# The products of a feed-forward block: from seven-for-eight float32 products to three float32r products of split parts

## The chip, the cores and the metric

The kernel runs on one core of a Trainium2 chip. The metric is device time in microseconds (us) from the start of the program to its end, the median of several executions. The core has a matrix engine (TensorE, in the profile PE, with its weight loads as PEld), a vector engine (VectorE, DVE), a scalar engine (ScalarE, ACT), a general engine (GpSimd, POOL) and a queue that issues most of the transfers (SyncE, SP). Each engine takes its own instructions strictly in the order in which they were written; engines wait for each other through semaphores.

## The reference

```
attn_out = mamba2_ssd(x, a, B, C)       # (4, 8, 768, 32): batch, heads, tokens, head dim
x = attn_out.transpose(0, 2, 1, 3).reshape(3072, 256)
h = maximum(maximum(x @ w1, x @ w2), x @ w3)     # w: 256 x 768
return h @ w_out                                 # w_out: 768 x 256
```

The first line is a decaying state-space scan with a state of 16 per head, in float32. The other lines are a feed-forward block (FFN) with a maximum over three products. The four FFN weights arrive as float64, so the kernel reads each as two 32-bit words per value and puts a float32 together from them ("decoding").

## The kernel before, in words

The 768 tokens of each batch are cut into six blocks of 128; with four batches a block has 4 x 128 = 512 columns (`BLK`). Blocks are called 0 to 5 here (`c` in the code). The program is unrolled and its order is written out by hand: `tc.manual_schedule()` keeps every instruction where the code puts it, and the strings `FIRST` (block 1), `STEADY` (blocks 2 to 4) and `LAST` (block 5) are plans of one word per action. While the FFN of block c runs, the plan weaves the scan of block c+1 between its products: transposes of B and C, scores (`s`), their product with the decay matrix L (128x512 multiplies on VectorE, in the list `later`, run by a digit in the plan), exponentials of L on ScalarE (words with x and z), masks of L on GpSimd (m and n), the state (A) and the scan's output y.

The FFN of block 0 uses plain float32 products of the three weights with `yT`, 512 columns each, while the weights are still being fetched and decoded. `decode()` begins with one weight part (two ScalarE, two VectorE, one GpSimd operation), `sign()` ends it (VectorE).

From block 1 on the code uses max(a1, a2, a3) = a2 + max(a1 - a2, a3 - a2, 0). `weight_sums` replaces w1 and w3 by their differences to w2 (`DIFF`, `BASE`); the a2 part goes through w2 and w_out at once: `fold_base` multiplies w2 by w_out into a 256x256 matrix, and the down product adds y times that matrix (`terms`). For the two differences, six pairs of weight columns (q = 0 to 2, i = 0 or 1) are each multiplied with y by a seven-for-eight (Strassen) scheme: `early` makes four products of 256 columns in PSUM banks sumA and sumB and the sums that follow, `late` three more, and the maxima. `weight_sums` and `scan_sums` prepare the sums of weights and of y that the seven products need.

`down_next` makes a quarter of the down product of half a block per call: for a group of 128 tokens eight terms (six of h with w_out, two of y with the folded matrix), 256 columns each; two groups share a bank, ScalarE copies it and SP sends it off. The down steps of block c run during block c+1, and the last block's are made by `last_next` at the end.

The words of a plan that matter here: E and L are early and late, D a down step, l a step of the last block's, a digit takes that many multiplies from `later`, y makes the scan's output, g and G turn and fold w2.

Of the kernel before, what the change touches and what calls it, by code (L numbers as in the profile page):

```python
# [11 lines left out]
U32 = mybir.dt.uint32  # L12
AF = mybir.ActivationFunctionType
# [6 lines left out]
def kernel(  # L20
# [39 lines left out]
    HB = BLK // 2  # L60
    MASKED = -32768.0
# [4 lines left out]
    raw = ctx.enter_context(tc.tile_pool(name="raw", bufs=2))  # L66
    att = ctx.enter_context(tc.tile_pool(name="att", bufs=2))
    ffn = ctx.enter_context(tc.tile_pool(name="ffn", bufs=2))
    wraw = ctx.enter_context(tc.tile_pool(name="wraw", bufs=10))
    wtmp = ctx.enter_context(tc.tile_pool(name="wtmp", bufs=3))  # L70
# [3 lines left out]


# [6 lines left out]
    def sum_bank(kind, shape):  # L82
        return bank("sum" + kind, {"A": 1, "B": 2}[kind], shape, "sum" + kind)

    def att_bank(shape, name):
        turn["att"] += 1
        if shared["att"] and turn["att"] % 5 == 0:
            return bank("sumA", 1, shape, name)
        return bank("att", 4, shape, name)

    def ffn_bank(shape, name):
        turn["ffn"] += 1
        if shared["ffn"] and turn["ffn"] % 3:
            return bank("sumB", 2, shape, name)
        return bank("ffn", 1, shape, name)

# [25 lines left out]
    def load(c, name):  # L122
        src, w = sources[name]
        t = blocks[c][name] = raw.tile([P, BH, w], FP32, tag="raw_" + name, name="raw_" + name)
        nc.sync.dma_start(
            out=t, in_=src[:, :, c * P:(c + 1) * P, :].rearrange("b h s n -> s (b h) n"))
# [3 lines left out]
    w_sb = [const.tile([P, KD, DF], FP32, name="w%d" % i) for i in range(3)]  # L130
    wo_sb = const.tile([P, NF, DM], FP32, name="wo")
# [5 lines left out]
    weight_jobs = []  # L137
    for f0 in range(0, DF, WCOL):
        for w, t in zip((moe_w1, moe_w2, moe_w3), w_sb):
            per = 1 if w.dtype == FP32 else 2  # L140
            src = words(w)[:, per * f0:per * (f0 + WCOL)]
            weight_jobs.append(
                (t[:, :, f0:f0 + WCOL], src.rearrange("(k p) f -> p k f", p=P), w.dtype))
    for o in range(0, NF, 2):
        weight_jobs.append(
            (wo_sb[:, o:o + 2],
             words(moe_w_out)[o * P:(o + 2) * P, :].rearrange("(o p) m -> p o m", p=P),
             moe_w_out.dtype))
# [3 lines left out]
    def fetch():  # L152

        dst, src, dt = weight_jobs.pop(0)
        if dt == FP32:
            nc.sync.dma_start(out=dst, in_=src)
        else:
            rb = wraw.tile([P, 2, WCOL, 2], U32, tag="rb", name="rb")
            nc.sync.dma_start(out=rb.rearrange("p k f w -> p k (f w)"), in_=src)
            fetched.append((dst, rb))  # L160

    def decode_steps():


        dst, rb = fetched.pop(0)
# [4 lines left out]
        def first():  # L170
# [3 lines left out]
            held["u"] = u = wtmp.tile(shape, U32, tag="w_u", name="w_u")  # L174
# [8 lines left out]
            r = wtmp.tile(shape, U32, tag="w_r", name="w_r")  # L183
# [3 lines left out]
        def second():  # L187
            nc.vector.scalar_tensor_tensor(  # L188
                out=dst.bitcast(U32), in0=hi.rearrange("p (k f) -> p k f", k=2),
                scalar=0x80000000, in1=held["u"].rearrange("p (k f) -> p k f", k=2),  # L190
                op0=ALU.bitwise_and, op1=ALU.bitwise_or)
# [184 lines left out]
    def last_load(c):  # L376
        E = blocks[c]["E"] = raw.tile([HN, NB, P], FP32, tag="E", name="E")
# [22 lines left out]
    def scan_b(c, kind):  # L400
# [4 lines left out]
        st["BT"] = BT = att.tile([HN, NB, P], FP32, tag="BT", name="BT")  # L405
# [13 lines left out]
    def scan_c(c):  # L419
# [3 lines left out]
        st["CT"] = CT = att.tile([HN, NB, 2, P], FP32, tag="CT", bufs=1, name="CT")  # L423
# [7 lines left out]
    def scan_cd(c):  # L431
# [3 lines left out]
        st["Cd"] = Cd = att.tile([HN, NB, P], FP32, tag="Cd", name="Cd")  # L435
        nc.vector.tensor_tensor(out=Cd, in0=st["trC"], in1=E, op=ALU.mult)

    def scan_bd(c):
        st = blocks[c]
        st["Bd"] = Bd = att.tile([P, BH, N], FP32, tag="Bd", name="Bd")  # L440
# [83 lines left out]
    def first_own(bs):  # L524
# [9 lines left out]
        if 0 not in yT:  # L534
            yT[0] = ffn.tile([P, KD, BLK], FP32, tag="yT", bufs=3, name="yT")
# [3 lines left out]

    def scan_y(c):  # L540
        yT[c] = ffn.tile([P, KD, BLK], FP32, tag="yT", bufs=3, name="yT")
        for t in range(KD):
            nc.scalar.copy(out=yT[c][:, t], in_=blocks[c]["y"][t].rearrange("p b i -> p (b i)"))

    def scan_sums(c):

        y11, y12, y21, y22 = (
            yT[c][:, k, r * HB:(r + 1) * HB] for k in range(2) for r in range(2))
        late = [blocks[c]["y"][k].rearrange("p b i -> p (b i)")[:, r * HB:(r + 1) * HB]
                for k in range(2) for r in range(2)]  # L550
        t = ysum[c % 2]
        later.extend(
            lambda k=k, a1=a1, a0=a0: nc.vector.tensor_tensor(
                out=t[:, k], in0=a1, in1=a0, op=ALU.subtract)
            for k, (a1, a0) in enumerate((
                (late[1], y11), (late[3], t[:, 0]), (late[3], y12), (late[2], t[:, 1]))))
        sides[c] = {1: y11, 2: y21, 3: y22, 4: t[:, 3], 5: t[:, 0], 6: t[:, 1], 7: t[:, 2]}


    hT = {}  # L560
    def h_of(c):
        if c not in hT:
            hT[c] = ffn.tile([P, NF, BLK], FP32, tag="h", name="h")
        return hT[c]

    def group(bank, i, f, halves):

        for r in halves:
            for k in range(KD):
                nc.tensor.matmul(  # L570
                    out=bank[:, r * HB:(r + 1) * HB],
                    lhsT=w_sb[i][:, k, f * P:(f + 1) * P],
# [3 lines left out]
    def whole_group(bank, i, f):  # L576
        for k in range(KD):
            nc.tensor.matmul(  # L578
                out=bank, lhsT=w_sb[i][:, k, f * P:(f + 1) * P], rhs=yT[0][:, k],
# [11 lines left out]
    NW = len(DIFF) * NQ  # L591
    ysum, wsum = [], {}

    def kilos(b):

        t = wraw.tile([P, 2, WCOL, 2], U32, tag="rb", name="rb").bitcast(FP32)
        return t.rearrange("p k f w -> p (k f w)").rearrange("p (a b) -> p a b", b=b)

    quarters = {}

    def places():
        for _ in range((NW + 1) // 2):
            t = kilos(P)
            for half in (t[:, 0:4], t[:, 4:8]):
                if len(wsum) < NW:
                    wsum[len(wsum)] = half
        ysum.extend(kilos(HB) for _ in range(2))

    def weight_sums(k):
        q, i = divmod(k, 2)  # L610
        w = w_sb[DIFF[i]]
        cols = slice(2 * q * P, 2 * (q + 1) * P)
        nc.vector.tensor_tensor(  # L613
            out=w[:, :, cols], in0=w[:, :, cols], in1=w_sb[BASE][:, :, cols], op=ALU.subtract)
        a11, a12, a21, a22 = (
            w[:, kk, (2 * q + g) * P:(2 * q + g + 1) * P]
            for g in range(2) for kk in range(2))
        s1, s2, s3, s4 = (wsum[k][:, j] for j in range(4))
        nc.gpsimd.tensor_tensor(out=s1, in0=a21, in1=a22, op=ALU.add)  # L619
        nc.gpsimd.tensor_tensor(out=s3, in0=a11, in1=a21, op=ALU.subtract)  # L620
        nc.gpsimd.tensor_tensor(out=s2, in0=s1, in1=a11, op=ALU.subtract)  # L621
        nc.gpsimd.tensor_tensor(out=s4, in0=a12, in1=s2, op=ALU.subtract)

    def left(p, k):
        if p in (1, 2, 4):
            q, i = divmod(k, 2)
            g, row = {1: (0, 0), 2: (0, 1), 4: (1, 1)}[p]
            f = 2 * q + g
            return w_sb[DIFF[i]][:, row, f * P:(f + 1) * P]
        return wsum[k][:, {5: 0, 6: 1, 7: 2, 3: 3}[p]]  # L630

    def products(c, k, which, first):
        for p, bank, half in which:
            nc.tensor.matmul(  # L634
                out=bank[:, half], lhsT=left(p, k), rhs=sides[c][p],
                start=(first and half == 0), stop=True, skip_group_check=True)
# [8 lines left out]
    held = {}  # L645

    def early(c, k):
        q, i = divmod(k, 2)
        A, B = (sum_bank(kind, [P, 2, HB]) for kind in "AB")
        products(c, k, [(1, A, 0), (6, A, 1), (5, B, 0), (7, B, 1)], True)  # L650
        if i == 0:
            held["m"] = ffn.tile([P, 4, HB], FP32, tag="m", name="m")

        if i > 0 and q % 2 not in quarters:
            quarters[q % 2] = kilos(HB)[:, 0:3]
        t = held["m"][:, 1:4] if i == 0 else quarters[q % 2]
        eu = wtmp.tile([P, 2, HB], FP32, tag="w_u", name="eu")
        v = wtmp.tile([P, 2, HB], FP32, tag="w_r", name="v")[:, 0]
        nc.scalar.copy(out=eu[:, 0], in_=A[:, 0])  # L659
        nc.vector.tensor_tensor(out=eu[:, 1], in0=A[:, 1], in1=eu[:, 0], op=ALU.add)  # L660
        nc.vector.tensor_tensor(out=v, in0=B[:, 1], in1=eu[:, 1], op=ALU.add)
        nc.vector.tensor_tensor(out=t[:, 2], in0=B[:, 0], in1=v, op=ALU.add)
        held["open"] = A, B, eu, t

    def late(c, k):
        q, i = divmod(k, 2)
        m = held["m"]
        A, B, eu, t = held.pop("open")
# [394 lines left out]
```

## Time and profile before

| what | us |
|---|---|
| three runs | 281.45, 283.35, 286.68 (median 283.35) |
| profiled execution, its span | 281.2 |
| TensorE busy in it | 267.4 (95%) |
| VectorE, ScalarE, GpSimd busy | 159.0, 116.6, 67.2 |
| block 0 (with the start), block 1 | 59.9, 46.4 |
| blocks 2, 3, 4 | 40.9, 40.9, 40.6 |
| block 5 with the end | 52.5 |

The time of the profiled execution itself is known by its span alone. The borders of the blocks are those between the first up products in TensorE's timeline. A line of the groups reads: line of the kernel, engine, operation, what it writes and reads, shapes, number of records; then busy time, mean duration of one in ns, idle time of the engine before them and what ended it. A float32 matmul leaves two records, one for each half of its weights. Neighbouring matmuls overlap in the records, so the cost of one is read from the distance of starts. Their mean duration is longer than that.

### The profile page before, as it was taken

How to read it: one execution, taken by the hardware profiler on the slowest of the kernel's cores; microseconds unless marked ns; L12 is line 12 of the kernel's file. 1: busy time of each engine (PE TensorE's matmuls, PEld its weight loads, DVE VectorE, ACT ScalarE, POOL GpSimd, SP SyncE). 2: the span in 40 equal slices, each digit the busy share in tenths (PEclk: the TensorE clock that was granted, in tenths of full speed). 3: DMA queues.
4: the chain of work that ended last, by engine and by line, in shares of the span. 5: the costliest groups of instructions: out<-in, count | busy, mean ns of one | idle time of the engine just before them, and what ended most of it. 6: DMA issues, size and time to landing. Idle time of an engine off the chain costs nothing.

```text
span 281.2 us, 4990 instructions
## 1 busy us (share of the span) xinstructions
PE 267.4 (95%) x1930; PEld 209.6 (75%) x1930; DVE 159.0 (57%) x298; ACT 116.6 (41%) x304; POOL 67.2 (24%) x84
## 2 busy tenths in 40 slices
PE   6889999989989999999999999999999999999994
PEld 4665344467767888877888868888878888888873
DVE  2585778989877342475643576634477534524320
ACT  2776588835756157332274332456231111100101
POOL 5163665457837400005200005100000000000000
PEclk9999999999999999997999999999999999999999
DMA  7989989989789408692005795001010001010012
GB/s 84 194 277 286 281 144 170 168 229 206 165 201 123 63 0 216 171 135 45 0 2 161 207 123 70 2 1 40 0 37 1 2 0 40 0 37 2 0 37 75
DMA packets 105047, 28.10 MB, mean 100 GB/s; under 512 B 75328, under 2 KB 101952, under 8 KB 105024
## 3 DMA queue, kind: packets, MB, share of 16 engines
q1 hardware_dynamic: 104144, 27.14, 48.4%
q10 hardware_dynamic: 880, 0.66, 0.7%
q8 instruction: 15, 0.25, 0.4%
q14 instruction: 8, 0.07, 0.1%
HBM read 24.54 MB, written 3.24 MB: 99 GB/s over the span
## 4 chain that ended last, share of the span: by engine, by line
PE 80%; DVE 13%; POOL 2%; ACT 2%; issue 2%; POOLq 0%; DVEq 0%; ACTq 0%
PE o L741 21%; PE sumB L634 16%; PE sumA L634 14%; PE up L578 6%; PE o L762 5%; PE s L483 5%; DVE L L491 4%; PE y L519 3%; PE fold L713 2%; PE y L506 1%; PE up L570 1%; PE spread L320 1%; DVE m L676 1%; DVE w_u L176 1%; DVE w L613 1%
## 5 line engine op out<-in xcount | busy, mean ns | idle before, releaser
L741 PE MATMUL o<-wo,h 128*128 128x256 f32 x240 | 58.4, 379 | 0.0
L391 ACT ACTIVATE L<-L,ncums 128x128 f32<-128x128 f32 x160 | 50.0, 392 | 7.1 <-POOL L L384 7.1
L741 PEld LDWEIGHTS o<-wo,h 128*128 128x128 f32 x240 | 45.5, 190 | 6.2
L659 ACT COPY eu<-sumA 128x256 f32<-128x256 f32 x30 | 11.2, 372 | 76.5 <-PE sumA L634 76.5
L660 DVE TENSOR_TENSOR eu<-sumA,eu 128x256 f32<-128x256 f32 x30 | 12.7, 424 | 52.5 <-ACT eu L659 52.5
L634 PE MATMUL sumA<-yT,w 128*128 128x256 f32 x120 | 37.5, 394 | 0.0
L491 DVE TENSOR_TENSOR L<-s,L 128x512 f32<-128x512 f32 x46 | 29.3, 681 | 2.9 <-PE s L483 2.9
L634 PE MATMUL sumB<-rb 128*128 128x256 f32 x120 | 30.8, 379 | 0.0
L578 PE MATMUL up<-yT,w 128*128 128x512 f32 x64 | 29.1, 600 | 0.2 <-DVE w L188 0.2
L634 PEld LDWEIGHTS sumA<-yT,w 128*128 128x128 f32 x120 | 21.7, 192 | 5.5 <-issue 1.4
L634 PEld LDWEIGHTS sumB<-rb 128*128 128x128 f32 x120 | 23.0, 192 | 3.2
L384 POOL TENSOR_SCALAR_AFFINE_SELECT L<-L 128x1024 f32<-128x1024 f32 x20 | 23.5, 1206 | 0.0
L578 PEld LDWEIGHTS up<-yT,w 128*128 128x128 f32 x64 | 11.6, 190 | 14.7 <-issue 11.7
L483 PE MATMUL s<-CT,BT 32*128 32x256 f32 x192 | 19.6, 403 | 3.1 <-DVE L L491 1.7
L185 POOL TENSOR_TENSOR w_u<-w_u,w_r 128x512 uint32<-128x512 uint32 x12 | 15.6, 1299 | 28.2 <-DVE w_u L179 14.6
L634 PE MATMUL sumA<-rb 128*128 128x256 f32 x60 | 18.4, 389 | 1.3 <-POOL rb L619 1.3
L483 PEld LDWEIGHTS s<-CT,BT 32*128 32x128 f32 x192 | 12.1, 184 | 10.0 <-issue 6.4
L634 PE MATMUL sumB<-yT,rb 128*128 128x256 f32 x60 | 18.1, 383 | 0.7 <-POOL rb L621 0.4
L634 PE MATMUL sumB<-rb,w 128*128 128x256 f32 x60 | 17.8, 379 | 0.0
L741 PE MATMUL o<-rb,yT 128*128 128x256 f32 x64 | 16.4, 379 | 0.0
L676 DVE TENSOR_TENSOR m<-sumB,eu 128x512 f32<-128x512 f32 x15 | 10.3, 688 | 10.6 <-PE sumB L634 10.5
L746 ACT COPY ob<-o 128x512 f32<-128x512 f32 x10 | 5.8, 583 | 21.6 <-PE o L741 21.6
(112 smaller groups left out, 365.8 us busy)
## 6 DMA issues: line engine op xcount, KB each, us to landing
L<-cums SPq DMA_DIRECT2D x10, 1024.0 KB, 9.3
rb<-in_moe_w_dram SPq DMA_DIRECT2D x9, 512.0 KB, 6.3
raw_x<-in_x_dram SPq DMA_DIRECT2D x6, 512.0 KB, 7.4
out_dram<-ob SPq DMA_DIRECT2D x10, 256.0 KB, 2.5
raw_B<-in_B_dram SPq DMA_DIRECT2D x6, 256.0 KB, 4.5
raw_C<-in_C_dram SPq DMA_DIRECT2D x6, 256.0 KB, 6.4
rb<-in_moe_w_out_dram SPq DMA_DIRECT2D x3, 512.0 KB, 6.1
E<-cums SPq DMA_DIRECT2D x40, 32.0 KB, 4.0
```

Source lines behind the costliest of these rows:

```text
L185: nc.gpsimd.tensor_tensor(out=u, in0=u, in1=r, op=ALU.add)
L384: nc.gpsimd.affine_select(out=Ls[c][:, b], in_=Ls[c][:, b], pattern=[[0, NH], [1, P]], compare_op=ALU.is_ge, fill=MASKED, base=0, channel_ ...
L391: nc.scalar.activation(L[:, b, h], L[:, b, h], AF.Exp, bias=ncum[c][:, b * NH + h:b * NH + h + 1], scale=1.0)
L483: nc.tensor.matmul(out=s[:, i].rearrange("j g i -> j (g i)"), lhsT=st["BT"][rows, b], rhs=st["CT"][rows, b].rearrange("p g i -> p (g i)"), ...
L491: nc.vector.tensor_tensor(out=M, in0=s, in1=M, op=ALU.mult)
L578: nc.tensor.matmul(out=bank, lhsT=w_sb[i][:, k, f * P:(f + 1) * P], rhs=yT[0][:, k], start=(k == 0), stop=(k == KD - 1))
L634: nc.tensor.matmul(out=bank[:, half], lhsT=left(p, k), rhs=sides[c][p], start=(first and half == 0), stop=True, skip_group_check=True)
L659: nc.scalar.copy(out=eu[:, 0], in_=A[:, 0])
L660: nc.vector.tensor_tensor(out=eu[:, 1], in0=A[:, 1], in1=eu[:, 0], op=ALU.add)
L676: nc.vector.tensor_tensor(out=t[:, 0:2], in0=B, in1=eu[:, 1:2].to_broadcast([P, 2, HB]), op=ALU.add)
L741: nc.tensor.matmul(out=o[:, i], lhsT=left_[:, b * P:(b + 1) * P], rhs=right_, start=(z == 0), stop=(z == 2 * n - 1), skip_group_check=True)
L762: nc.tensor.matmul(out=o[:, b % 2], lhsT=left_[:, b * P:(b + 1) * P], rhs=right_, start=(z == 0 and b % 2 == 0), stop=True, skip_group_che ...
```

## The change

From block 1 on (the second block) every FFN product is made of three products in the type float32r. Writing a float32r tile rounds each value to fewer mantissa bits. A value v is split in a near part H = v (1 - 2^-13), so rounded, and the rest L = v - H, both float32r. With R = 4096 and the weights' rest scaled by R, the bank first takes Hw·Hy + R Lw·Ly; it is multiplied in place by 1 + 1/R; then (Lw - Hw/R)·(Hy - R Ly) is added. What is left is Hw·Hy + Lw·Ly + Lw·Hy + Hw·Ly, all four terms. The third factors are called S, and made by one VectorE operation each.

The Strassen scheme with its sums goes. A unit is now one of six columns f and one of two differences i: twelve units per block (`NU`), with 4 + 2 products of 512 columns. The bank of a unit is scaled on ScalarE (even units) or VectorE (odd), copied by ScalarE (i = 0) or compared by VectorE (i = 1), and h is split by VectorE and GpSimd. The weights' differences, w_out and the folded matrix are split once, in 42 steps (`back`) spread over block 0 and block 1. A down step now is one term and one of its three parts for all four token groups (four products), 24 per block, begun at unit 9 of the own block. Block 0 stays in float32, with its down product now in `first_down` (block 1).

Besides, all working tiles come from two pools of equal tiles (61 of 2 KB and 10 of 4 KB per partition), PSUM has two banks for up, two for o and four for the scan, and some transfers are moved: four weight fetches, the E rows and x of block 1 go from ahead of block 0's products to between them, and the loads of block 2 from n = 3 to n = 11 of block 0's loop.

```diff
+    halves = ctx.enter_context(tc.tile_pool(name="halves", bufs=61))
+    wholes = ctx.enter_context(tc.tile_pool(name="wholes", bufs=10))
...
     def scan_y(c):
+        y_parts[c] = tuple(whole([P, KD, BLK], "y" + n, F32R) for n in "HLS")
+        ys = [t.rearrange("p b i -> p (b i)") for t in blocks[c]["y"]]
+        H, L, S = y_parts[c]
+        for k in range(KD):
+            nc.scalar.mul(H[:, k], ys[k], NEAR)
+
+        def far(k):
+            nc.vector.tensor_tensor(
+                out=L[:, k], in0=ys[k], in1=plain(H)[:, k], op=ALU.subtract)
+
+        steps = [lambda k=k: far(k) for k in range(KD)]
+        return steps + [
+            lambda k=k: crossed(S[:, k], plain(H)[:, k], plain(L)[:, k]) for k in range(KD)]
+
+    def crossed(out, H, L):
+        nc.vector.scalar_tensor_tensor(
+            out=out, in0=L, scalar=-RAISE, in1=H, op0=ALU.mult, op1=ALU.add)
...
+    def split_steps(src, rest, parts):
+        shape = [P, 2, WCOL]
+        H, L, S = (half(shape, "w" + n, F32R) for n in "HLS")
+        parts += [H, L, S]
+        eng = nc.gpsimd if rest is not None and src.space != PSUM else nc.vector
+
+        def lower():
+            nc.scalar.mul(L, rest, RAISE)
+
+        return [
+            lambda: nc.scalar.mul(H, src, NEAR),
+            lambda: eng.tensor_tensor(out=rest, in0=src, in1=plain(H), op=ALU.subtract),
+            lower,
+            lambda: nc.vector.scalar_tensor_tensor(
+                out=S, in0=plain(H), scalar=-1.0 / RAISE, in1=rest, op0=ALU.mult, op1=ALU.add),
+        ]
...
+    def near_far(bank, c, u):
+        f, i = divmod(u, 2)
+        q, g = divmod(f, 2)
+        for z in range(2):
+            for k in range(KD):
+                nc.tensor.matmul(
+                    out=bank, lhsT=up_parts[q, i][z][:, k, g * P:(g + 1) * P],
+                    rhs=y_parts[c][z][:, k], start=(z == 0 and k == 0),
+                    stop=(z == 1 and k == KD - 1), skip_group_check=True)
+
+    def raise_sum(bank, eng):
+        if eng is nc.scalar:
+            nc.scalar.mul(bank, bank, 1.0 + 1.0 / RAISE)
+        else:
+            nc.vector.tensor_scalar(
+                out=bank, in0=bank, scalar1=1.0 + 1.0 / RAISE, scalar2=None, op0=ALU.mult)
+
+    def early(c, u):
+        up = up_bank([P, BLK], "up")
+        near_far(up, c, u)
+        raise_sum(up, nc.vector if u % 2 else nc.scalar)
+        opened.append((c, u, up))
+
+    def late():
...
+        c, u, up = opened.pop(0)
...
+        for k in range(KD):
+            nc.tensor.matmul(
+                out=up, lhsT=up_parts[q, i][2][:, k, g * P:(g + 1) * P],
+                rhs=y_parts[c][2][:, k], start=False, stop=(k == KD - 1), skip_group_check=True)
         if i == 0:
+            held["m"] = m = half([P, BLK], "m")
+            nc.scalar.copy(out=m, in_=up)
+            cross_next()
+            return
+        h = half([P, BLK], "h")
         nc.vector.scalar_tensor_tensor(
+            out=h, in0=up, scalar=0.0, in1=held["m"], op0=ALU.max, op1=ALU.max)
+        H, L = (half([P, BLK], "h" + n, F32R) for n in "HL")
+        h_parts[c][f] = [H, L]
+        nc.vector.tensor_scalar(out=H, in0=h, scalar1=NEAR, scalar2=None, op0=ALU.mult)
+        nc.gpsimd.tensor_tensor(out=L, in0=h, in1=plain(H), op=ALU.subtract)
+        crossings.append((c, f))
...
+    TERMS = [("h", 0), ("h", 1), ("h", 2), ("h", 3), ("y", 0), ("y", 1), ("h", 4), ("h", 5)]
+
+    def queue_downs(c):
+        for t in TERMS:
+            downs.extend((c, t, z) for z in range(2))
+        downs.extend((c, t, 2) for t in TERMS)
...
+        products(c, o, term, z, range(NB), first)
+        if term == TERMS[-1] and z == 1:
+            raise_sum(o[0], nc.scalar)
+            raise_sum(o[1], nc.vector)
...
     FIRST = [
+        "Z sign tc b2 load m01",
+        "Z p sign g c e b2 q",
+        "Z p 1 x2 g m23 b2 q q",
+        "Z p x2 q b2",
+        "Z p s0 x1 b2 q",
+        "Z p 4 x2 g b3 q",
+        "Z p x1 s2 b3 n01 q",
+        "Z p 4 A b2 q",
+        "Z p 1 G6 b4",
+        "Z p G6 z2 b4 d d",
+        "Z p y b4 d 2 d",
+        "Z p 2 n23 z3 d d",
     ]
     STEADY = [
+        "Z p x1 d d load",
+        "Z p t d d",
+        "Z p c e d d x1",
+        "Z p 1 s0 d d 2",
+        "Z p d 2 d x1 n01",
+        "Z p d s2 d 2",
+        "Z p d 2 d A",
+        "Z p 1 d y d z1",
+        "Z p 2 d d 2",
+        "Z p z1 n23 d d",
+        "Z p d d z1",
+        "Z p d d z2",
     ]
     LAST = [
+        "Z p d d d", "Z p d d d", "Z p d d d", "Z p d d d", "Z p d d d", "Z p d d d",
+        "Z p l l l", "Z p l l l", "Z p l l l", "Z p l l", "Z p l l", "Z p l l",
     ]
```

In the new plans Z is `early` of the unit, p is `late` of the unit before, d a down step of parts, q a float32 down step of block 0, b runs split steps. `last_next` (l) makes the last block's down steps in separate banks for near and cross parts and adds them at the end.

More of the change, by code (lines that the diff above doesn't have):

```diff
@@ L624, in left @@
[L624 to L636, printed above, removed]
+    up_parts, down_parts, fold_parts = {}, {}, []
@@ new lines, in wo_steps, with nth, step, paired @@
+    def wo_steps(o):
+        state = {}
+        def nth(n):
+            def step():
+                if n == 0:
+                    down_parts[o] = []
+                    state["rest"] = split_steps(
+                        wo_raw[o], half([P, 2, WCOL], "d"), down_parts[o])
+                state["rest"][n]()
+            return step
+        return [nth(n) for n in range(4)]
+    def paired(one, two):
+        order = (0, 0, 1, 1, 2, 3, 2, 4, 3, 4)
+        which = (0, 1, 0, 1, 0, 0, 1, 0, 1, 1)
+        return [(one, two)[w][o] for w, o in zip(which, order)]
@@ L638, with behind @@
+    back = []
+    def behind(n):
+        while n and back:
+            back.pop(0)()
+            n -= 1
     later = []
@@ L682, in raised @@
[L682 to L695 removed]
+    h_parts = {c: {} for c in range(NC)}
```

435 lines of the change are left out of this document (204 added, 231 removed).

## The prediction

> **What bounds the kernel now.** I read the page's busy shares first, then the chain that ended last, the costliest groups, TensorE's timeline, and busy time by stretches cut at the blocks' borders.
>
> ```profile
> PE 267.4 (95%) x1930; PEld 209.6 (75%) x1930; DVE 159.0 (57%) x298; ACT 116.6 (41%) x304; POOL 67.2 (24%) x84
> PE 80%; DVE 13%; POOL 2%; ACT 2%; issue 2%; POOLq 0%; DVEq 0%; ACTq 0%
> L741 PE MATMUL o<-wo,h 128*128 128x256 f32 x240 | 58.4, 379 | 0.0
> L741 PEld LDWEIGHTS o<-wo,h 128*128 128x128 f32 x240 | 45.5, 190 | 6.2
> L578 PE MATMUL up<-yT,w 128*128 128x512 f32 x64 | 29.1, 600 | 0.2 <-DVE w L188 0.2
> L676 DVE TENSOR_TENSOR m<-sumB,eu 128x512 f32<-128x512 f32 x15 | 10.3, 688 | 10.6 <-PE sumB L634 10.5
> L746 ACT COPY ob<-o 128x512 f32<-128x512 f32 x10 | 5.8, 583 | 21.6 <-PE o L741 21.6
> ```
>
> TensorE owns 80% of the chain, and the other engines wait for it. The next view, busy time by stretches (block 1, blocks 2 to 4), says how tightly:
>
> ```profile
> 59.90:106.30 46.40, 43.31 (x335) 35.10 (x334) 31.68 (x58) 24.18 (x71) 26.59 (x36) 1.00 0.65 124
> 106.30:147.20 40.90, 40.33 (x309) 33.43 (x309) 21.36 (x42) 18.04 (x53) 6.58 (x7) 0.96 0.53 98
> 147.20:188.10 40.90, 40.33 (x317) 33.78 (x316) 22.83 (x44) 17.01 (x49) 5.52 (x6) 1.00 0.52 97
> 188.10:228.70 40.60, 40.02 (x286) 33.54 (x285) 22.50 (x43) 11.07 (x29) 0.00 (x0) 1.00 0.04 14
> ```
>
> The columns are length, then PE, PEld, DVE, ACT and POOL busy, clock and DMA. In blocks 2 to 4 TensorE is busy for all but 0.6 us of 41; VectorE is at 55%, ScalarE at 43%. So the price of a change is the price of TensorE's columns, until another engine's queue holds it up. Block 5 takes 228.7 to 281.2, 52.5 us; block 0 ends at 59.9.
>
> What a column costs is read from the timeline of TensorE (start, length, group):
>
> ```profile
> 205.10 1.89 PE L741 MATMUL o<-wo,h 128*128 128x256 f32 x8
> 42.08 0.60 PE L410 MATMUL trC<-ident,raw_C 128*128 128x128 f32 x4
> 2.50 1.87 PE L304 MATMUL spread<-mask,ident 128*128 128x512 bf16 x4 [2.50 <-POOL mask L241]
> ```
>
> and from the groups of TensorE by shape:
>
> ```profile
> L332 PE MATMUL spread<-npick,a 32*128 32x512 f32 x8 | 1.9, 999 | 0.0
> ```
>
> Eight float32 records of 256 columns: (1.89 - 0.379)/7 = 0.216 us apart, 2 cycles per column at the full clock. A float32 product is two records (240 in this group, for 120 products in the code), so 0.432 us: four cycles per column. The bfloat16 products of 512 columns at the start are (1.87 - 0.62)/3 = 0.42 us apart, as slow per column. But TensorE ran slowly there: a float32 record of 512 columns lasted 999 ns at 6 us and 600 later, so a column took (999 - 600)/512 = 0.8 ns more, twice the later 0.83, though the clock column shows 1.00 (2.40 to 4.40 us). At that half rate 0.42 us is 1 cycle per column.
>
> **TensorE's sum.** Before, a block from 1 to 5 has 42 up products (6 pairs x 7) and 32 down products (4 token groups x 8 terms) of 256 columns: 18.13 + 13.81 = 31.94 us. Five blocks: 159.7 us. The rest of a steady block, 40.9 - 31.9 = 9.0 us, is the scan's matmuls and transposes, which stay.
>
> After, a block has 12 up units x 6 products of 512 columns and 24 down steps x 4 products of 256: in units of 256 columns 144 + 96 = 240, five blocks 1200. No row shows a float32r product. The lower end is 1 cycle per column, 0.108 us (bfloat16's row, and half a float32 record); the upper end 2 cycles, 0.216 us (the float32 records and the transposes, which are single records and still (0.60 - 0.275)/3 = 0.108 us apart for 128 columns). I take 0.108: a float32 record's two cycles go to the two halves of its moving operand, and this operand has one. Five blocks: 129.5 us, 30.2 less. Break-even, before any stall, is 159.7/1200 = 0.133 us, 1.23 cycles per column.
>
> The Trainium skill speaks against this: "SBUF — State Buffer", section "A bandwidth-pool intuition that's wrong (but worth ruling out)", gives TensorE's moving operand 2 bytes per lane and cycle; by that, a 4-byte column takes two cycles, and the five blocks 259 us. The transposes' row agrees with it, the float32 rows fit both readings. It is the first rival below.
>
> **Weight loads.** They must hide behind 0.108 us. The float32 loads last 190 ns each and do hide: the products behind them are 0.216 us apart, which is bare streaming. Loads of 32 columns last 110 ns and of 128 columns 190, so 0.83 ns per column above a fixed 83; the transposes' single loads last 141, so 58 ns of streaming. 58 is below 108, so I cost them at nothing; uncovered they cost 58 ns each.
> The Trainium skill, "TensorE: Matmul & The Clock Gate", section "The mechanism", says that loads overlap running matmuls only when their row groups differ; these loads use all rows and overlap, so this trace disagrees, and I give it the second half of that rival only.
>
> **The in-place scaling and the splits**, per steady block (36 us), by rows of 128x512: from PSUM 0.58 us on ACT and 0.69 on DVE, in SBUF about 0.6 on ACT, 0.43 to 0.64 (single source) or 0.69 (two) on DVE, 1.3 on POOL. Writing PSUM is in no row; I take the same, bounds 0.4 and 1.0.
> DVE: 6 scalings, 6 maxima, 6 near parts, 6 cross parts = 6 x (0.69+0.69+0.5+0.7) = 15.5; y's far and cross 2.8; scores 8 x 0.68 = 5.4; down 1.4; Cd and state 1.1: 26.2 us, 73%. ACT: 6 x 1.17 + 2.4 for y and output + 10 exponentials' busy time + 2.6 for the scan = 22 us, 61%. POOL: 6 x 1.3 + 4.8 of masks + 2.6 = 15 us. None becomes the bound on average.
>
> The waits are in the order. There are two "up" banks. Unit u's first four products (0.86 us) need the bank that unit u-2 left, evacuated after its last two products (0.43 us). Between these lie two down steps (0.86 us) and some scan. The evacuation takes 0.6 to 0.7 us plus some 0.1 of signalling: just covered if ACT or DVE is free when it is due. What stands before it there is two score multiplies (1.4 us on DVE) or four exponentials (1.25 us on ACT). With a hand-traced pair of units DVE runs without a gap while the eight score multiplies fall, and TensorE waits 0.1 to 0.5 us per pair. Everything on TensorE queues behind that wait, down products too. The scaling itself has a whole unit (some 2 us) and is hidden; down's scaling has the next unit's up products before it. I take 1.5 us per steady block (0 to 4). Blocks 2 to 4: 40.8 - 6.0 + 1.5 = 36.3 each, 108.9.
>
> **Block 0** keeps its float32 products and decoding. Weight 6 is fetched behind B and C of block 1, whose issues hold SP's queue from 28.3 to 35.5 us; it was issued from 20.9 to 28.2 together with two others, and will be some 5 us later, landing near 37. Its decoding begins near 36. ACT would stand there with its exponentials behind it. POOL gets four subtractions (5.2 us) into idle time of 15 us. The Strassen weight sums (DVE 1.1, POOL 1.8 per pair), for which TensorE waited 1.3 us at the border, go. What is late next there is y's far part: two ACT and one to two DVE operations, 2 us after y's last product, of which 1.6 lie beside other products. Net +1 us (0 to 4): 60.9.
>
> **Block 1** loses 2.6 us of up products and gains six down steps (6 x 0.432 = 2.6): nothing. But ACT has about 40 us of work here (16 split steps 10, 13 exponential parts 16, scalings and copies 7, the rest), 85%, and the chains run POOL, ACT, DVE in turn behind POOL's masks, which wait for decays that landed near 72 us. I take +1.1 (0 to 6): 47.5.
>
> **Block 5**: nine units of 2.59 us (up 1.30, three steps 1.29) and three of 2.16: 29.8; the last unit's two products 0.4. Then h must pass maximum 0.7, near 0.5, far on POOL 1.3, cross 0.7 and four handoffs: 4 us, of which other down products cover 2.6. Then 0.9 of products, 0.9 for the last addition, and from there 3.1 to the end (before: last product 278.0, end 281.2). With 0.5 of stalls 39.6, against 52.5.
>
> Sum: 60.9 + 47.5 + 108.9 + 39.6 = **256.9 us** against 281.2. The profiled execution's span is 0.25 below the lowest of the three runs and 2.2 below their median; I add 1: **258**.
>
> **Rivals.**
> 1. Slower: a one-pass product does not stream a column per cycle. It decides from 0.133 us per 256 columns on. At two cycles 1200 x 0.108 = 129.5 us are added to 258: some 380. If instead the 58 ns loads lie uncovered, 5 x (72 + 96) x 0.058 = 49 us: some 300. For it: the transposes' row. Against: hidden float32 loads, bfloat16's row. Chances 0.13 and 0.06.
> 2. The queues take the gain: DVE at 73% and ACT at 85% in block 1 hold the two banks. Steady blocks at 39, block 1 at 52, block 0 at 63: 63 + 52 + 117 + 41 = 273, with the 1 us 274. For: three scalings or copies per pair on in-order engines. Against: these engines idle over 40% now. Chance 0.12, within 266 to 277.
> 3. All of it and slow weights, 277 to 289, no change that a measurement of this kernel can tell (about 2%): 0.06.
> 4. No stalls at all: 251 less, below 249: 0.03.
>
> My forecast, 249 to 266, has 0.60. Faster 0.60 + 0.12 + 0.03 = 0.75, same 0.06, slower 0.19. The range 247 to 289 holds 0.8.
>
> **What would show it.** Float32r records: one per product, 0.108 us apart at 256 columns and 0.216 at 512, loads near 141 ns. Blocks near 36 us, TensorE's waits on the bank's evacuation (DVE h, ACT m) under 2 us per block. Records 0.2 us apart make the forecast wrong at once; records as forecast with blocks of 39 would be rival 2.

## The result, and the profile after

The changed kernel takes 293.3 us (292.1 to 295.0), the kernel before 285.0 beside it: a ratio of 1.038, with an interval of 1.029 to 1.047. It is slower; I had forecast 258. Some executions of every kernel here take some per cent longer at a lower granted clock, and the ratios leave them out. The profiled execution's span is 292.6 us.

The page's busy shares and chain, after:

```profile
PE 257.2 (88%) x2030; PEld 197.6 (68%) x2030; DVE 177.7 (61%) x283; ACT 144.6 (49%) x336; POOL 117.9 (40%) x105
PE 54%; DVE 19%; DMA 6%; SPq 5%; ACT 5%; POOL 4%; issue 4%; POOLq 1%; DVEq 0%; ACTq 0%
```

TensorE's share of the chain fell from 80% to 54%. Its busy time fell by 10 us where I had 30 less, and it now waits. Busy time by stretches says where: block 0's products, block 1, blocks 2 to 4, block 5 (length, then PE, PEld, DVE, ACT, POOL, clock, DMA).

```profile
18.90:68.80 49.90, 42.69 (x287) 22.16 (x287) 36.54 (x57) 31.83 (x73) 26.40 (x22) 0.97 0.89 194
68.80:129.00 60.20, 49.89 (x350) 38.33 (x347) 34.29 (x51) 35.56 (x89) 35.69 (x29) 0.93 0.62 124
129.00:169.80 40.80, 37.63 (x333) 31.09 (x333) 27.77 (x43) 19.49 (x49) 15.18 (x13) 0.97 0.46 84
169.80:210.85 41.05, 37.84 (x339) 31.14 (x338) 26.41 (x41) 20.72 (x54) 15.18 (x13) 1.00 0.37 63
210.85:249.50 38.65, 36.89 (x305) 30.47 (x305) 23.41 (x39) 16.77 (x39) 7.76 (x6) 1.00 0.04 15
249.50:292.60 43.10, 38.01 (x243) 34.04 (x241) 19.00 (x32) 9.28 (x16) 9.01 (x7) 0.99 0.08 25
```

| part | before | forecast | after | missed by |
|---|---|---|---|---|
| block 0 with the start | 59.9 | 60.9 | 68.8 | 7.9 |
| block 1 | 46.4 | 47.5 | 60.2 | 12.7 |
| blocks 2 to 4 | 122.4 | 108.9 | 120.5 | 11.6 |
| block 5 with the end | 52.5 | 39.6 | 43.1 | 3.5 |

The clock column differs too. This is the clock granted to TensorE in tenths of full speed, over the span in 40 slices of 7 us, before and after:

```profile
PEclk9999999999999999997999999999999999999999
PEclk9999999799999879979999999999999999999999
```

In the kernel before TensorE was granted a clock of 0.50 once, for 3.4 us from 127.2; in the changed kernel four times for as long, from 52.7, 93.7, 103.9 and 127.8 us. It had work all through these stretches, so each cost it up to 1.7 us of full speed: 6.8 us against 1.7, of which 1.7 fall in block 0, 4.0 in block 1 and 1.1 in block 2. (The half clock after the last product costs nothing.) In the 3.4 us ahead of each of the four TensorE had stood for 2.9, 2.2, 1.7 and 2.0 us, ahead of the one before for 0.6. In all profiles of this case, cut along the clock's own steps of 3.4 us, every step after the first product in which TensorE stood for 2 us or more was followed by one at half clock; with less it was so now and then. That a long wait costs a second time in this way is thus likely, but no run changes the clock by itself.

The products themselves, in TensorE's timeline in block 5, where no scan runs beside them:

```profile
250.81 0.63 PE L811 MATMUL o<-wH,hH 128*128 128x256 f32 x4
251.75 0.64 PE L811 MATMUL o<-wH,yH 128*128 128x256 f32 x4
252.23 0.63 PE L692 MATMUL up<-yH,wH 128*128 128x512 f32 x2
252.69 0.62 PE L692 MATMUL up<-yL,wL 128*128 128x512 f32 x2
```

One record per product now. From start to start, over the whole of this stretch, four of 256 columns take 0.478 us, 0.1195 each; two of 512 take 0.465, 0.2325 each. That is 11% above the 0.108 and 8% above the 0.216 that I took.

And the waits that are new, from the view of who waited for whom (us in total, times, longest):

```profile
ACT wL L622 <- POOL d L626: 14.2, 5, 4.5
DVE wS L628 <- POOL d L626: 13.4, 5, 4.2
ACT w_u L191 <- DMA rb<-in_moe_w_dram: 6.7, 3, 3.7
PE s L501 <- ACT CT L443: 6.0, 2, 4.6
PE up L692 <- ACT m L722: 3.0, 2, 1.7
```

ScalarE and VectorE stand 27.6 us at GpSimd's subtraction `d`, the rest of a weight part (`split_steps`). For block 0 I had no such term, for block 1 one of 1.1 us. Two stretches of the timeline show what stands behind them. In block 0:

```profile
47.35 1.26 POOL L201 TENSOR_TENSOR w_u<-w_u,w_r 128x512 uint32<-128x512 uint32 x1 [0.89 <-DVE w_u L195]
48.58 1.26 POOL L626 TENSOR_TENSOR d<-d,wH 128x512 f32<-128x512 f32 x1
49.87 0.63 ACT L622 ACTIVATE wL<-d 128x512 fp32r<-128x512 f32 x1 [3.23 <-POOL d L626]
50.87 1.27 ACT L443 ACTIVATE CT<-trC,parity 128x512 f32<-128x512 f32 x2
52.19 1.62 PE L501 MATMUL s<-CT,BT 32*128 32x256 f32 x16 [4.64 <-ACT CT L443]
```

GpSimd makes `d` after a decoding step; ScalarE waits 3.2 us for it with CT queued behind, and TensorE waits 4.6 us for CT. In block 1:

```profile
119.75 1.29 POOL L626 TENSOR_TENSOR d<-w,wH 128x512 f32<-128x512 f32 x1 [6.30 <-ACT wH L625]
121.07 0.69 DVE L628 SCALAR_TENSOR_TENSOR wS<-wH,d 128x512 fp32r<-128x512 f32 x1 [4.19 <-POOL d L626]
121.68 0.68 DVE L726 SCALAR_TENSOR_TENSOR h<-up,m 128x512 f32<-128x512 f32 x1
122.42 0.73 PE L692 MATMUL up<-yH,wH 128*128 128x512 f32 x2 [1.24 <-DVE h L726]
```

VectorE waits 4.2 us for `d`, behind it stands the maximum that empties an up bank, and TensorE waits for that bank.

### The profile page after: what moved, and what is told of

Same layout as the page of the kernel before. It is cut to its first block, busy times and chain, and to the rows that moved or that the text cites. A ratio compares the mean times of both kernels' runs of the same rounds, so it can differ in the third digit from the quotient of the medians.

```text
span 292.6 us, 5239 instructions
## 1 busy us (share of the span) xinstructions
PE 257.2 (88%) x2030; PEld 197.6 (68%) x2030; DVE 177.7 (61%) x283; ACT 144.6 (49%) x336; POOL 117.9 (40%) x105
## 4 chain that ended last, share of the span: by engine, by line
PE 54%; DVE 19%; DMA 6%; SPq 5%; ACT 5%; POOL 4%; issue 4%; POOLq 1%; DVEq 0%; ACTq 0%
PE up L692 15%; PE o L811 14%; PE up L717 7%; PE s L501 4%; SPq L173 3%; PE o L792 3%; DVE L L509 2%; DVE yS L577 2%; PE up L597 2%; DMA rb<-in_moe_w_dram 2%; DMA raw_C<-in_C_dram 2%; SPq L139 2%; DVE h L726 2%; PE y L537 2%; DVE yL L569 2%
## 5 line engine op out<-in xcount | busy, mean ns | idle before, releaser
L731 POOL TENSOR_TENSOR hL<-h,hH 128x512 fp32r<-128x512 f32 x30 | 39.0, 1299 | 121.4 <-DVE hH L730 106.7
L726 DVE SCALAR_TENSOR_TENSOR h<-up,m 128x512 f32<-128x512 f32 x30 | 20.7, 691 | 49.8 <-PE up L717 34.7
L692 PE MATMUL up<-yH,wH 128*128 128x512 f32 x120 | 42.6, 437 | 4.2 <-ACT m L722 3.0
L717 PE MATMUL up<-yS,wS 128*128 128x512 f32 x120 | 38.7, 404 | 3.0 <-DVE up L701 2.9
L692 PE MATMUL up<-yL,wL 128*128 128x512 f32 x120 | 39.2, 407 | 1.8 <-DVE yL L569 1.7
L722 ACT COPY m<-up 128x512 f32<-128x512 f32 x30 | 17.5, 584 | 40.6 <-PE up L717 40.3
L701 DVE TENSOR_SCALAR up<-up 128x512 f32<-128x512 f32 x30 | 20.9, 695 | 18.4 <-PE up L692 18.4
L717 PEld LDWEIGHTS up<-yS,wS 128*128 128x128 f32 x120 | 22.6, 192 | 9.9 <-DVE up L701 4.4
L692 PEld LDWEIGHTS up<-yL,wL 128*128 128x128 f32 x120 | 23.3, 194 | 8.6 <-DVE yL L569 3.2
L577 DVE SCALAR_TENSOR_TENSOR hS<-hL,hH 128x512 fp32r<-128x512 f32 x30 | 23.4, 782 | 1.5 <-POOL hL L731 1.5
L811 PE MATMUL o<-wH,hH 128*128 128x256 f32 x120 | 21.1, 294 | 1.1 <-DVE ob L839 1.1
```

The lines of the kernel that those rows point to most:

```text
L577: nc.vector.scalar_tensor_tensor(out=out, in0=L, scalar=-RAISE, in1=H, op0=ALU.mult, op1=ALU.add)
L692: nc.tensor.matmul(out=bank, lhsT=up_parts[q, i][z][:, k, g * P:(g + 1) * P], rhs=y_parts[c][z][:, k], start=(z == 0 and k == 0), stop=(z ...
L701: nc.vector.tensor_scalar(out=bank, in0=bank, scalar1=1.0 + 1.0 / RAISE, scalar2=None, op0=ALU.mult)
L717: nc.tensor.matmul(out=up, lhsT=up_parts[q, i][2][:, k, g * P:(g + 1) * P], rhs=y_parts[c][2][:, k], start=False, stop=(k == KD - 1), skip ...
L726: nc.vector.scalar_tensor_tensor(out=h, in0=up, scalar=0.0, in1=held["m"], op0=ALU.max, op1=ALU.max)
L731: nc.gpsimd.tensor_tensor(out=L, in0=h, in1=plain(H), op=ALU.subtract)
```

## The experiments

Profiles are compared by distances inside an execution, because the start differs: in five of the ten profiles below TensorE's granted clock is 0.50 for 10.2 us from some 16 us on, and the first product of 512 columns comes some 5 us later. The distances are from block 0's first product of 512 columns to block 1's first up product ("block 0"), from there to the scan's output y in block 2 ("block 1"), and from that y to the next (a steady block). The last column is what TensorE lost to half clock in the distances of block 0 and block 1, at most (half the time at 0.50); in the two steady blocks it lost nothing in any run. A difference in block 0 or 1 that is no larger than the difference in that column can be the clock's alone.

| kernel | block 0 | block 1 | steady blocks | lost to half clock |
|---|---|---|---|---|
| the changed kernel | 45.1 | 85.5 | 40.8, 40.3 | 1.7, 5.1 |
| B and C fetched later | 44.4 | 84.0 | 40.8, 40.2 | 3.4, 3.4 |
| no rests on GpSimd | 39.4 | 76.6 | 40.9, 40.2 | 0, 0 |
| rests on VectorE | 41.4 | 81.2 | 40.9, 40.3 | 1.7, 3.4 |
| splits in a pipeline | 40.4 | 84.6 | 40.9, 40.3 | 0, 3.4 |
| the same, steady plan moved | 40.0 | 83.7 | 38.0, 37.4 | 0, 5.1 |
| bfloat16 parts | 44.5 | 81.7 | 38.6, 38.0 | 3.4, 1.7 |
| no scaling | 44.4 | 79.3 | 39.2, 38.6 | 3.4, 0 |
| rests on VectorE, steady plan moved | 41.6 | 77.7 | 38.0, 37.4 | 0, 0 |
| the same, lower parts on GpSimd | 41.4 | 78.2 | 38.0, 37.4 | 1.7, 1.7 |

### Was it the late weight?

```diff
-    fetch()
-    load(1, "B")
-    load(1, "C")
     decode()
...
+        if n == 2:
+            load(1, "B")
+            load(1, "C")
```

> The changed kernel, with B and C of block 1 fetched after weight 7 (the order of the kernel before) instead of ahead of weight 6. Theory T1: block 0 is 8.9 us longer because ScalarE stands 3.7 us at weight 6, which the longer queue delivers late, and everything behind it (CT, the scores) is late by it; then block 0 falls from 68.8 to about 64, and the time by 4 to 5 us, from 293 to about 288.5. Rival R1: block 0 is longer because the split steps hold ScalarE (3.2 us at GpSimd's rest of the difference); then the weight comes earlier, the wait for it goes, and block 0 loses less than 1.5 us.

Ratio to the kernel before 1.026 (1.016 to 1.036), which overlaps that of the changed kernel. The wait for weight 6 is gone, and the one behind it in TensorE (for the sign of that weight, 1.8 us) is down to 0.3; the wait of 4.6 us for CT is still there, and block 0 is only 0.7 us shorter. That is R1's number, but TensorE also lost 1.7 us more to half clock here, behind that wait for CT: at an equal clock the late weight would be worth up to 2.4 us. So T1's 4 to 5 us are not reached, and the late weight that I had named was real and is the smaller part of block 0's loss; between 0.7 and 2.4 this run does not decide.

### The rests of the weight parts

Without GpSimd's subtraction:

```diff
-            nc.scalar.mul(L, rest, RAISE)
+            nc.scalar.mul(L, src, RAISE)
...
-            lambda: eng.tensor_tensor(out=rest, in0=src, in1=plain(H), op=ALU.subtract),
+            lambda: None,
...
-                out=S, in0=plain(H), scalar=-1.0 / RAISE, in1=rest, op0=ALU.mult, op1=ALU.add),
+                out=S, in0=plain(H), scalar=-1.0 / RAISE, in1=src, op0=ALU.mult, op1=ALU.add),
```

> The changed kernel without the subtraction that makes the rest of each weight part; L and S are made from the whole value instead. It leaves out 9 GpSimd subtractions and one on VectorE (about 12 us of GpSimd), and with them the waits of ScalarE (14.2 us) and VectorE (13.4 us) for them; ScalarE and VectorE do as many operations as ever. Theory T2: in block 1 and at the end of block 0 the in-order queues standing at these waits hold the two up banks, and TensorE loses its 10 us of idle time to them; then block 1 falls from 60.2 to about 50 and block 0 by some 3, the time to about 280. Rival R2: block 1 is long because ScalarE and VectorE have too much work there (35.6 and 34.3 us busy) and the products are dearer; then it stays above 57 and the time above 289.

284.5 us (I had 280), ratio 1.000 (0.994 to 1.005): 5.7 us less in block 0, 8.9 in block 1, with ScalarE and VectorE as busy as ever. This is block 1 in this run, in the columns of the stretches above:

```profile
68.00:119.30 51.30, 44.86 (x350) 36.13 (x349) 35.42 (x50) 34.32 (x85) 26.77 (x22) 1.00 0.58 116
```

So 14.6 of the missed 35.7 us hang on these subtractions, and not on the work of ScalarE and VectorE. They do so in two ways. For the same 350 records TensorE is busy 44.9 us instead of 49.9, at a clock of 1.00 instead of 0.93, and it stands 6.4 us instead of 10.3: 5.0 of the 8.9 us are a longer busy time (up to 4.0 of it the half clock) and 3.9 are waits, where T2 had waits alone. Whether the subtractions act by the waits behind them or by GpSimd's load, the next runs ask. First the rests on VectorE:

```diff
-        eng = nc.gpsimd if rest is not None and src.space != PSUM else nc.vector
+        eng = nc.vector
```

> The changed kernel with the weights' rests subtracted on VectorE (0.69 us) instead of GpSimd (1.3 us): all work is kept, VectorE gets 6 us more of it. T2: the chain behind a split then crosses from ScalarE to VectorE and back only, so ScalarE's 14.2 us and VectorE's 13.4 us of waits fall to a few, block 1 falls to about 52, the time to about 283. R2 (too much work): VectorE gets more, so block 1 stays at 60 or grows, the time is 293 or more.

286.7 us (I had 283), ratio 1.011 (1.004 to 1.019). All work is there, VectorE has more of it, and block 0 and 1 are 3.7 and 4.3 us shorter (1.7 of the 4.3 can be the clock): R2 falls. Part of the wait stays (ScalarE 6 to 9 us at VectorE's rest), so the gain is about half of that without the rests. Then all rests on GpSimd, but two other steps between a rest and what needs it:

```diff
+    ORDER = (
+        "d0 d1 h0 r0 h1 r1 d2 l0 s0 d3 l1 s1 "
+        "h2 r2 h3 r3 d4 d5 l2 s2 l3 s3 "
+        "h4 r4 h5 r5 h6 r6 l4 s4 l5 s5 "
+        "h7 r7 l6 s6 h8 r8 l7 s7 l8 s8")
+    back += [splits[int(t[1])]["dhrls".index(t[0])] for t in ORDER.split()]
```

> The changed kernel with all its work, but the 42 split steps in another order: at least two other steps stand between GpSimd's subtraction and the two operations that need it (the weight parts overlap as in a pipeline). T2 (the in-order queues of ScalarE and VectorE stand at GpSimd's rests): the two groups of waits, 14.2 and 13.4 us, fall below 5 each, block 0 is 4 to 5 us and block 1 some 7 us shorter, the time about 283. Rival R2b: the two runs with other rests were shorter because GpSimd had less to do (its port, its queue); GpSimd has all its work here, so the time stays at 290 or more.

289.2 us, ratio 1.026 (1.016 to 1.035): I had 283. The waits for GpSimd's rests are gone altogether, and block 0 is 4.7 us shorter with all of GpSimd's work: there it was the waits, R2b falls. But block 1 gains 0.9 us only, for my order made parts late for their first product. The timeline of this run:

```profile
108.88 2.43 ACT L409 ACTIVATE L<-L,ncums 128x128 f32<-128x128 f32 x8
111.21 0.61 ACT L622 ACTIVATE wL<-d 128x512 fp32r<-128x512 f32 x1
111.97 1.11 PE L811 MATMUL o<-wL,hL 128*128 128x256 f32 x4 [4.55 <-ACT wL L622]
```

The part stands behind eight exponentials and TensorE behind the part; with 2.5 us more at unit 4 that is 7 us, which eats the gain. So in block 1 this run does not tell the waits from GpSimd's load. The run with rests on VectorE does not either, for it takes that load off GpSimd; the last run below does.

### The price of a product

> Products alone, in series of 20 or 40 behind each other with four weight tiles in turn: float32r with 512, 256 and 128 columns, bfloat16 with 512 and 256, float32 with 256 and 512; nothing of the reference's work is done. Theory T3: a float32r product costs 0.232 us for 512 columns and 0.119 for 256 by itself (a column a cycle, and 10 to 19 ns for the load that isn't wholly hidden), bfloat16 0.216 and 0.108. Rival R3: the surplus comes from the other engines' use of memory beside it; then float32r alone shows 0.216 and 0.108.

The kernel runs series of products and nothing else, each series with loads of four weights in turn:

```python
        for i in range(count):
            j = 0 if same else i % 4
            nc.tensor.matmul(out=bank[:, 0:n], lhsT=wt[:, j * P:(j + 1) * P], rhs=mt[:, 0:n],
                             start=True, stop=True, skip_group_check=True)
```

Its groups by shape, r being float32r, b bfloat16, f float32:

```profile
L65 PE MATMUL r<-r_m,r_w 128*128 128x512 f32 x40 | 9.7, 400 | 0.0
L65 PE MATMUL f<-f_m,f_w 128*128 128x256 f32 x40 | 8.8, 379 | 0.0
L65 PE MATMUL b<-b_m,b_w 128*128 128x512 bf16 x39 | 8.6, 379 | 0.1
L65 PE MATMUL r<-r_m,r_w 128*128 128x128 f32 x40 | 5.0, 284 | 0.0
L65 PE MATMUL r<-r_m,r_w 128*128 128x256 f32 x40 | 5.0, 283 | 0.0
L65 PE MATMUL b<-b_m,b_w 128*128 128x256 bf16 x40 | 4.5, 272 | 0.0
```

```profile
L65 PEld LDWEIGHTS r<-r_m,r_w 128*128 128x128 f32 x120 | 17.1, 190 | 2.6 <-issue 1.0
L65 PEld LDWEIGHTS <-b_w 128*128 128x128 bf16 x80 | 7.8, 98 | 5.2
```

By (busy - one duration)/(count - 1): float32r 0.239, 0.121 and 0.121 us for 512, 256 and 128 columns; bfloat16 0.216 and 0.108. Nothing else runs, so R3 falls. Half the columns cost the same 0.121, so up to 256 columns something other than the columns sets the pace. The load of 190 ns is the likely one, but its length alone is not it: the float32 records of 256 columns have loads as long, stream as long as a float32r product of 512, and stand 0.216 us apart ((8.8 - 0.379)/39) where that stands 0.239. What about the type costs the 0.023 us, and whether a float32r product without a new load would be free of it, was not tried. Then the same in the kernel, with bfloat16 parts (the parts lose bits, the products and operations stay):

```diff
-F32R = mybir.dt.float32r
+F32R = mybir.dt.bfloat16
...
     def plain(t):
-        return t.bitcast(FP32)
+        return t
```

> The changed kernel with all split parts in bfloat16 instead of float32r: the same products, columns and operations, with shorter parts, so the output loses precision. T3 (a float32r product pays 10 to 19 ns beyond its columns for its 190 ns load): products of 512 and 256 columns stand 0.216 and 0.108 us apart, and a steady block falls by about 2 us, to 38.5 to 39, block 5 likewise. Rival R4b: the steady block is set by VectorE's queue, so it stays at 40 or more although the products are cheaper (some of VectorE's and GpSimd's operations may be faster on 2-byte data too).

281.9 us in one execution. Loads last 98 ns, products of 512 columns stand 0.216 us apart and of 256 0.109, and the steady blocks fall by 2.2 us, with VectorE's operations as long as before (0.68, 0.69, 0.45 us; the cross part is even longer, 0.84 against 0.78), GpSimd's rest of h somewhat shorter (1.17 against 1.30). T3's numbers hold: 72 x 0.0166 + 96 x 0.0116 = 2.3 us per block is what float32r costs beyond its columns, 11.6 in five blocks. That it is the load is argued, for the type changes with the load. R4b falls.

### What the steady blocks wait for

VectorE and GpSimd, at the border of two steady blocks of the changed kernel:

```profile
202.84 2.59 POOL L402 TENSOR_SCALAR_AFFINE_SELECT L<-L 128x1024 f32<-128x1024 f32 x2
203.17 2.81 DVE L577 SCALAR_TENSOR_TENSOR yS<-yL,yH 128x512 fp32r<-128x512 f32 x2
205.90 0.69 DVE L701 TENSOR_SCALAR up<-up 128x512 f32<-128x512 f32 x1
206.64 0.73 PE L717 MATMUL up<-yS,wS 128*128 128x512 f32 x2 [1.44 <-DVE up L701]
```

The two cross parts of y take 1.4 us each beside the masks, where the same operation on h took 0.68 without them. The scaling stands behind, and TensorE behind the scaling. (The Trainium skill, "SBUF — State Buffer", section "Who interferes with whom", has it that a VectorE operation with two inputs in SBUF contends with a GpSimd operation that reads SBUF; these rows agree.) Two moves in the plan, on top of the pipelined splits:

```diff
-        "Z p c e d d x1",
-        "Z p 1 s0 d d 2",
+        "Z p c e d d 1 x1",
+        "Z p s0 d d 2",
...
-        "Z p d 2 d A",
+        "Z p d 2 d A n23",
...
-        "Z p z1 n23 d d",
+        "Z p z1 d d",
```

> The one before with two more moves in the plan of blocks 2 to 4: the masks of the second half go from unit 9 to unit 6, away from the split of y on VectorE, and Cd (which frees the bank that the scores need) goes one unit earlier. Theory T4: the steady blocks of 40.8 us hold 28.2 us of products, 9.0 of scan and some 3 us of waits at VectorE (1.4 for the scaling behind y's splits, 1.0 for Cd, 0.8 for the o banks), of which these two go: steady blocks 38.5 to 39, the time 6 us below that of the run with pipelined splits alone. Rival R4: TensorE is bound by its own products there and the waits only show slack; then the steady block stays within 0.5 us of 40.8.

Steady blocks of 38.0 and 37.4 us, 2.9 less, and TensorE's waits in one are down to 0.8: T4 holds, R4 falls. With the masks elsewhere the two cross parts of y take 1.28 us together instead of 2.81. How much each of the two moves gives was not tried. The executions lie between 281.2 and 290.9 (median 287.1), too far apart for an interval; the block times are what this run shows. In such a block TensorE stands for 0.7 us only:

```profile
165.00:203.00 38.00, 37.26 (x338) 31.00 (x337) 24.97 (x40) 20.54 (x52) 15.26 (x14) 1.00 0.47 87
```

Without the in-place scaling:

```diff
-        if eng is nc.scalar:
-            nc.scalar.mul(bank, bank, 1.0 + 1.0 / RAISE)
+        if True:
+            return
```

> The changed kernel without the in-place scaling of the up and down banks: it leaves out 70 operations on ScalarE and VectorE (20 us and 24 us of busy time) and the waits for them. If the scaling holds TensorE (part of T4), the steady blocks fall from 40.8 to 38.5 or less and block 1 by 2 us or more; if its cost lies beside other work, as I forecast, the steady blocks stay within 1 us of 40.8 and only the 1.4 us wait per block goes.

282.6 us in one execution: steady blocks 1.6 us shorter, block 1 6.2. Neither number that I had set is met. In the steady blocks the wait of 1.4 us goes, others of 0.3 to 0.6 per block come in its place, so the scaling costs about what its wait shows. Of the 6.2 us in block 1 up to 5.1 can be the clock, which was never at half there in this run; what the scaling itself costs there stays open.

### A version that beats both

> All of the work of the changed kernel, with two mends: the weights' rests on VectorE (as in the third run) in the old order of steps, and the two moves in the plan of blocks 2 to 4. By T2 and T4 the gains add: block 0 and 1 as with rests on VectorE (41 and 56 us from the first product of 512 columns), steady blocks 38.0: the time 9 us below the 286.7 of the rests alone, 278; faster than the kernel before by 1 to 2%. If the gains overlap (steady blocks wait for something else then), 283 or more.

278.9 us, ratio 0.985 (0.979 to 0.992): 1.5% below the kernel before, 14 us below the changed one. Both gains are there, block by block, and in the profiled execution TensorE lost nothing to half clock in any block before the last products; up to 6.8 of the 14 us can be that. What waits in block 1 is now the transposes of w2 (2.6 us for VectorE's scores), the state's sums (1.9), and four waits for a bank or y's far part of 0.6 to 1.4 us.

```diff
-            nc.scalar.mul(L, rest, RAISE)
+            nc.gpsimd.tensor_scalar(
+                out=L, in0=rest, scalar1=RAISE, scalar2=None, op0=ALU.mult)
...
-        "Z p G6 z2 b4 d d",
+        "Z p G6 b4 z2 d d",
```

> The same, and the scaled rest of a weight part (L) is made on GpSimd, which the rests have left, instead of ScalarE; in unit 9 of block 1 the split steps stand ahead of the exponentials. ScalarE then waits in no split step. T2: block 1 falls by another 2 to 4 us, the time to about 275, 3% below the kernel before. If GpSimd's operation holds the masks and parts of h instead, no gain or a loss of 2 us.

278.6 us, ratio 0.985 (0.979 to 0.990): no different from the one before, where I had 275. ScalarE's waits for a rest are gone, VectorE's at ScalarE's near part (4.3 us) remain. GpSimd is now busy for 126.8 us in all, more than the 117.9 of the changed kernel, and block 1 is still 7.3 us shorter than there (3.9 with what half clock took in each left out). The plan moved for the steady blocks also reaches into this distance, but on the rests on VectorE it gave 3.5 us there, of which 3.4 can be the clock. So GpSimd's load by itself does not make block 1 long, and R2b falls there too.

## Why the prediction was wrong

**The columns: right.** Float32r streams its columns nearly as fast as bfloat16 (0.239 and 0.216 us for 512 in series), and rival 1 at two cycles a column (380 us) is out. The transposes' row, 0.108 us for 128 columns, was no measure for it. (The Trainium skill, "SBUF — State Buffer", section "A bandwidth-pool intuition that's wrong (but worth ruling out)", gives the 2 bytes per lane and cycle for bf16. Carried over to float32r, as in rival 1, they would make its 4-byte columns take twice bfloat16's time, 0.43 us for 512; 0.2325 was measured, so they are no limit for this type.)

**The weight loads: wrong.** "58 is below 108, so I cost them at nothing" was the step. I read the load's length from the transposes (141 ns), but a float32r load lasts 190 like a float32 one, and in series a product of 256 columns costs no less than one of 128, 0.121. A float32r product costs 0.0116 to 0.0166 us beyond its columns, most likely for its load. TensorE's saving was 159.7 - 5 x (72 x 0.2325 + 96 x 0.1195) = 18.6 us where the sum had 30.2. It is the half-hidden case between my forecast and the second half of rival 1, at 11.6 of its 49 us. (The Trainium skill, "TensorE: Matmul & The Clock Gate", section "Weight-path perf modes — Fast Weight Load (FWL) and DoubleRow", keeps the fast load for types other than FP32 and does not speak of float32r; 98 ns for bfloat16 against 190 for float32 agree, and float32r's 190 fit if it counts as FP32.)

**Block 0: wrong step.** "POOL gets four subtractions (5.2 us) into idle time of 15 us" counted GpSimd's time and not who stands waiting for it. ScalarE stood, with CT behind it. Without the rests, or with other steps between, 4.7 to 5.7 of the 7.9 us come back, with them the 1.7 us of half clock that followed the wait for CT. The step that I did fear, the late weight, is 0.7 of it, at most 2.4.

**Block 1: wrong size, mechanism half named.** I wrote that "the chains run POOL, ACT, DVE in turn", priced that at 1.1 us with 6 as the bound, and gave ScalarE's 85% as its reason. ScalarE was busy 59% of the block; it was the waits in the queue. 12.7 us were missed: 8.9 hang on the rests (3.9 as TensorE's standing, 5.0 as its longer busy time, most of it half clock), 1.5 are products, about 2 are not settled.

**The clock: no term.** The sum took full speed throughout. TensorE lost 6.8 us to half clock in the changed kernel's profile and 1.7 in that of the kernel before. These 5.1 us are inside the misses of blocks 0, 1 and 2, not beside them.

**Blocks 2 to 4.** The stalls of "1.5 us per steady block (0 to 4)" were 3.6 and 3.9 in blocks 2 and 3 (40.8 and 41.05 less 28.2 of products less 9.0 of scan), inside the bounds; the term that I left out is the doubling of VectorE's operations beside masks. Block 4, which has no masks, had 1.45, as forecast. With 2.3 per block for what float32r costs beyond its columns that makes the 11.6 us missed here. The scaling "is hidden" was wrong by some 1.6 us a block. The prices of the operations themselves were right: 0.582 and 0.695 us in place in PSUM, 0.69, 0.44 and 1.30 for h.

**Block 5** missed by 3.5, of which 2.3 are that price of float32r; the last chain after the last unit (283.0 to 292.6, with 8.9 forecast) took 9.6.

**Rival 2** had the right kind of cause and 273 us; with the 11.6 us of the products added it would have given 285. Its prices came from averages of busy time, and they could not show a queue that stands.

## What to carry to other kernels

An operation moved to an idle engine is not free if an in-order engine waits for it: what counts is the time until it is done, with everything queued on that engine before it, against the steps that stand between it and its reader; put several other steps there, but look at the reader's deadline as well. A long wait of TensorE can be followed by a stretch at half clock, so compare the clock column before a difference in time is put down to a change in the code. Price a product by a series of the type and the columns that are used: neither its columns (0.108 us for 256) nor its load (0.190) gave the 0.12 that was measured. With the two waits mended and the products as dear as they are, the three-product form wins, by 1.5% and not by the 9% that I had forecast.

## What the runs showed that I had not expected

A float32r product costs 0.121 us for 128 columns as for 256; its load lasts 190 ns, bfloat16's 98. Scaling a PSUM bank in place takes ScalarE 0.58 us and VectorE 0.70 for 512 columns, as long as copying it out. VectorE's cross parts, with two inputs in SBUF, took 1.4 us each while GpSimd's masks ran and 0.64 without them. TensorE ran at half clock for 3.4 us after every step of 3.4 us in which it had stood for 2 us or more.
